# Weights of a fused retention and MLP kernel: loaded as fp32 by one queue and cast by GpSimd, instead of cast in flight by GpSimd's own queue

## The chip, the cores and the metric

The kernel runs on one core of a Trainium2 chip. The metric is the device time of one execution in microseconds (us). A core has five engines with queues of their own: TensorE (PE: matrix products), VectorE (DVE), ScalarE (ACT), GpSimd (POOL) and SyncE (SP, which here only issues DMAs). Sixteen DMA engines move the data of all queues.

## What is computed

Retention (attention with a decay in place of softmax) over 8 batches of 8 heads, 576 positions and 64 channels, then an MLP on the 4608 tokens:

```python
scores = scale * np.matmul(q, k.transpose(0, 1, 3, 2))
Dmat = np.where(rel >= 0, gamma[:, None, None] ** rel[None, :, :], 0.0)   # rel = position of query - of key
ret = scores * Dmat[None, :, :, :]
x = np.matmul(ret, v)            # then transposed to 4608 tokens x 512
h = x @ w_in                     # 512 x 2048
g = h * np.cos(h)
out = g @ w_out                  # 2048 x 512
```

All inputs and the output are fp32.

## The kernel before, in words

The decay is split into factors on q and v, so that the retention of a chunk of 128 positions is a masked product within the chunk plus a product with a running state. Batches 0 and 1 are worked in chunks of each batch (4 of 128 and one of 64 positions); from token 1152 on the chunks run over the joined sequence and are numbered by `g`, from 9 to 35. The MLP goes over nine blocks of 512 tokens: `mlp1` multiplies x by 128 columns of w_in (four products), ACT takes the cosine (`cb`, L552), DVE multiplies (`gt`, L554); the second product goes through `plain2` (blocks 0 and 1) or `mlp2` (the others). All products that are not woven go through `group` (L461, and L463 for a group's last), the woven ones of the later chunks through `weave` (L709).

All orders are written out by hand in `emit`: the calls stand there in one list, and each engine gets its instructions in that order and works them strictly in order. A small recorder adds semaphore waits.

Loads of q, k and v go to a ring of 16 buffers `ld` (128 x 512 fp32) and are issued by SP (`fetch`, L290; `load_g`, L317). A list of loads, `pend`, says in which order; `pump` is called after each use of a buffer and issues the next loads as long as their buffers are free. The loads of a joined chunk `g` are also held back when more than `AHEAD` (9) buffers would be in use, or `AHEAD + 3` from a certain `g` on. SP issues, in the same queue, the DMA transposes of the later chunks (`turn_dma`, L390), which bring k and q (`kq`) into the layout `kqt` that the scores need. `prep(g)` makes POOL cast k and scale q and v of chunk `g` (`casts_g`), then emits the transpose, then pumps; so where loads stand against transposes in SP's queue is set by that limit. `visit(g)` is PE's work on chunk `g` and the scores of chunk `g + 1`.

In batches 0 and 1 the first four chunks' k and q come as "quads" (`quad`, a load with rows of 256 values), are cast or scaled to `qs` (`quad_cast`), turned on PE and copied to `kqt`. `back` turns k back to `kq`, `scores` and its mask give `rt`, `state_mm` and `state_copy` keep the state (`st`, copied to `sb`), `rest` multiplies with v (`vb`, scaled by `decay`, L378) and copies x to `xt`.

The weights are loaded by POOL's queue in eight DMAs of 128 x 4 x 512 values each, four for w_in (L330) and four for w_out (L336), which convert fp32 to bf16 on the way into `win` and `wout`. They stand between POOL's scalings of batch 0's v. SP's loads of batch 0's last chunk and of batch 1 wait, by `after`, until the second of these has been issued in the program's order.

`idle(n)` issues n products of zeros on PE whose result nobody reads.

Of the kernel before, what the change touches and what calls it, by code (L numbers as in the profile page):

```python
# [12 lines left out]
DFF = 2048  # L13
DM = H_ * D_
# [9 lines left out]
NL = 16  # L24
AHEAD = 9
# [8 lines left out]
def slot(b, r):  # L34
    return SLOT[(NCH * b + r) % NR]
# [108 lines left out]
class _Kernel:  # L144
# [179 lines left out]
        src = bass.AP(self.src[x], (b * H_ + 2 * c) * S_ * D_, [[4 * D_, 128], [S_ * D_, 2], [1, 4 * D_]])  # L324
        self.fetch((x, b, "c", c), src, [[4 * D_, 2], [1, 4 * D_]], 128)

    def w_in_load(self, g):
        dst = bass.AP(self.WIN, 512 * g, [[4 * DFF, 128], [DFF, 4], [1, 512]])
        src = bass.AP(self.w_in, 512 * g, [[DFF, 128], [128 * DFF, 4], [1, 512]])
        self.wtok[f"wi{g}"] = self.s.dma("pool", f"wi{g}", lambda e: e.dma_start(dst, src), writes=[self.bWIN[g]])  # L330

    def w_out_load(self, g):
        dst = bass.AP(self.WOUT, 4 * g * DM, [[16 * DM, 128], [DM, 4], [1, DM]])
        src = bass.AP(self.w_out, 4 * g * 128 * DM, [[DM, 128], [128 * DM, 4], [1, DM]])
        w = Buf()
        t = self.s.dma("pool", f"wo{g}", lambda e: e.dma_start(dst, src), writes=[w])  # L336
        for i in range(4 * g, 4 * g + 4):
            self.bWOUT[i].w = [t]
        self.wtok[f"wo{g}"] = t

    def copy(self, eng, o, x, reads, writes):
        fn = (lambda e: e.activation(o, x, AF.Copy)) if eng == "act" else (lambda e: e.tensor_copy(o, x))  # L342
# [540 lines left out]
    def pump(self):  # L883

        while self.pend:
            fn, a = self.pend[0]
            if fn == self.after:
                if a[0] not in self.wtok:
                    return
            else:  # L890
                n = 3 if fn == self.load_g or fn == self.load and len(a) == 2 else 1
                if any(self.busy[(self.n_ld + i) % NL] for i in range(n)):
                    return
                if fn == self.load_g and sum(self.busy) + n > (AHEAD if a[0] < 4 * 4 else AHEAD + 3):
                    return
            self.pend.pop(0)
            fn(*a)

# [6 lines left out]
    def emit(self):  # L905
        self.late = None
        self.pend, self.wtok = [], {}
        self.busy = [False] * NL
        for b in range(2):
            if b:  # L910
                self.push(self.after, "wi1")
                self.push(self.load, 0, 4)
            for c in range(NP):
                for x in "kq":
                    self.push(self.quad, x, b, c)
            for r in range(4):
                self.push(self.load, b, r, "v")
        self.push(self.load, 1, 4)
        for g in range(G0, NG):
            self.push(self.load_g, g)  # L920
# [3 lines left out]
        def m1(dts, o, j=0):  # L924
            for dt in dts:
                self.mlp1(j, dt, *o)

        self.idle(10)
        for c in range(NP):
            for x in "kq":  # L930
                i = self.quad_cast("pool" if x == "k" else "dve", x, 0, c)
                self.pump()
                self.quad_turn(x, 0, c, i, "act")
                self.idle(2 if c else 1)
        self.s.need("pool", [self.wtok["v", 0, 0]])
# [7 lines left out]
        for r in range(4):  # L943
# [40 lines left out]
        def pairs(t):  # L984
            return [(t[i], int(t[i + 1])) for i in range(0, len(t), 2)]

        for n in range(16):
            self.plain2(0, n % 4, n // 4, None)
            if n == 3:
                self.turn(0, 4, "k", "act", PS)  # L990
                self.turn(0, 4, "q", "act", SS)
            if n == 4:
                self.scores(0, 4)
            if n == 6:
                self.rest(0, 4)
# [67 lines left out]
        for j in range(2, NTB):  # L1063
            g = 4 * j + 4 if j < NTB - 1 else NG
# [42 lines left out]
```

## Time and profile before

| | |
|---|---|
| median of 3 runs | 296.93 us (296.46 to 298.5) |
| the profiled execution | 299.12 us, span of its instructions 297.4 us |
| granted TensorE clock | 1.00 |
| busy, PE / DVE / ACT / POOL | 285.3 / 214.6 / 173.9 / 95.6 us |
| bytes read from HBM / written | 36.70 / 9.44 MB |
| weight loads, issue to landing (median) | w_in 10.2 us, w_out 17.0 us |

Times in the profile count from the span's start. A row of a time line has start, duration, engine, line, operation, result and sources, shape, how many instructions were merged, and in brackets the idle time of the engine just before and what ended it. "SPq" and "POOLq" rows are issues of DMAs: their duration is that of the issue, not of the transfer. A row of busy times by stage has the stage, then for each engine its busy time and, in brackets, its number of instructions, then the granted clock, the mean number of busy DMA engines as a share of 16 (over 1 where packets overlap), and GB/s. A row of the waits has the waiting engine and line, whom it waited for, the total, how many times, and the longest.

### The profile page before, as it was taken

How to read it: one execution, taken by the hardware profiler on the slowest of the kernel's cores; microseconds unless marked ns; L12 is line 12 of the kernel's file. 1: busy time of each engine (PE TensorE's matmuls, PEld its weight loads, DVE VectorE, ACT ScalarE, POOL GpSimd, SP SyncE). 2: the span in 40 equal slices, each digit the busy share in tenths (PEclk: the TensorE clock that was granted, in tenths of full speed). 3: DMA queues.
4: the chain of work that ended last, by engine and by line, in shares of the span. 5: the costliest groups of instructions: out<-in, count | busy, mean ns of one | idle time of the engine just before them, and what ended most of it. 6: DMA issues, size and time to landing. Idle time of an engine off the chain costs nothing.

```text
span 297.4 us, 8336 instructions
## 1 busy us (share of the span) xinstructions
PE 285.3 (96%) x3526; PEld 180.6 (61%) x3558; DVE 214.6 (72%) x465; ACT 173.9 (58%) x344; POOL 95.6 (32%) x120
## 2 busy tenths in 40 slices
PE   6899999999998999999999999999999999999996
PEld 2465455655553568646864785478547854785485
DVE  3667848568567688579857985798579757956973
ACT  6688624797347664566457535753586358535720
POOL 3580237754426430580058006700670030000000
PEclk9999999999999999999999999999999999999999
DMA  6999999999999999999999965899591170013013
GB/s 202 230 200 193 197 330 182 270 228 181 210 227 236 186 202 215 251 203 182 207 237 224 197 150 145 174 228 166 153 200 5 37 143 3 2 36 108 0 37 106
DMA packets 142325, 49.70 MB, mean 167 GB/s; under 512 B 125904, under 2 KB 141264, under 8 KB 142288
## 3 DMA queue, kind: packets, MB, share of 16 engines
q1 hardware_dynamic: 129280, 35.53, 67.3%
q10 hardware_dynamic: 8784, 9.44, 9.9%
q0 software_dynamic: 4224, 4.19, 8.7%
q8 instruction: 28, 0.46, 0.7%
q14 instruction: 9, 0.07, 0.1%
HBM read 36.70 MB, written 9.44 MB: 155 GB/s over the span
## 4 chain that ended last, share of the span: by engine, by line
PE 84%; DMA 9%; issue 2%; SPq 2%; DVE 1%; ACT 1%; DVEq 0%
PE mm L461 56%; PE mm L463 19%; DMA ld<-in_q_dram 3%; PE st L709 3%; PE sc L709 2%; DMA win<-in_moe_w_in_dram 2%; DMA ld<-in_v_dram 2%; DMA kqt<-kq 2%; SPq L290 2%; PE po L709 2%; PE sc L461 1%; PE po L461 1%; PE st L461 0%; PE sc L463 0%; ACT cb L552 0%
## 5 line engine op out<-in xcount | busy, mean ns | idle before, releaser
L554 DVE TENSOR_TENSOR gt<-mm,cb 128x512 bf16<-128x512 f32 (+3 forms) x156 | 99.4, 647 | 35.0 <-ACT cb L552 34.0
L552 ACT ACTIVATE cb<-mm,c_pih 128x512 bf16<-128x512 f32 (+3 forms) x156 | 100.7, 654 | 37.3 <-PE mm L463 36.4
L461 PE MATMUL mm<-xt,win 128*128 128x512 bf16 (+3 forms) x446 | 113.4, 362 | 3.1 <-issue 1.9
L461 PEld LDWEIGHTS mm<-xt,win 128*128 128x128 bf16 x468 | 43.5, 98 | 45.2 <-DVE gt L554 0.8
L463 PE MATMUL mm<-xt,win 128*128 128x512 bf16 (+3 forms) x156 | 56.6, 363 | 0.1
L342 POOL CAST kq<-ld 128x512 bf16<-128x512 f32 (+1 forms) x29 | 17.7, 610 | 117.4 <-PE mm L463 100.6
L461 PE MATMUL mm<-wout,gt 128*128 128x256 bf16 (+1 forms) x256 | 49.1, 309 | 1.0 <-issue 0.8
L461 PE MATMUL mm<-ts,ss 128*128 128x256 bf16 x240 | 35.4, 273 | 0.0
L461 PEld LDWEIGHTS mm<-wout,gt 128*128 128x128 bf16 x264 | 24.7, 98 | 11.8 <-DVE gt L554 0.5
L342 ACT ACTIVATE u<-mm 128x512 f32<-128x512 f32 x21 | 12.5, 597 | 32.3 <-PE mm L463 32.3
L365 POOL TENSOR_TENSOR vb<-ld,wv 128x512 bf16<-128x512 f32 x27 | 28.4, 1052 | 6.4 <-DMA ld<-in_v_dram 4.0
L361 POOL TENSOR_TENSOR kq<-ld,uq 128x512 bf16<-128x512 f32 x27 | 28.2, 1044 | 4.3 <-DMA ld<-in_q_dram 4.3
L342 ACT ACTIVATE xt<-po 128x256 bf16<-128x256 f32 (+1 forms) x35 | 14.6, 418 | 23.0 <-PE st L709 15.7
L463 PE MATMUL mm<-wout,gt 128*128 128x256 bf16 (+1 forms) x88 | 27.4, 311 | 0.1
L643 DVE TENSOR_TENSOR osb<-mm,u 128x512 f32<-128x512 f32 x20 | 13.8, 688 | 18.8 <-PE mm L463 11.2
L750 DVE TENSOR_TENSOR rt<-sc,mh 128x256 bf16<-128x256 f32 x54 | 21.2, 416 | 5.9 <-PE st L709 2.5
L463 PEld LDWEIGHTS mm<-xt,win 128*128 128x128 bf16 x156 | 15.3, 98 | 16.0
L461 PEld LDWEIGHTS mm<-ts,ss 128*128 128x128 bf16 x240 | 23.0, 98 | 2.8
L463 PE MATMUL mm<-ts,ss 128*128 128x256 bf16 x80 | 21.8, 272 | 0.0
L576 DVE TENSOR_TENSOR ss<-gt 128x512 bf16<-128x512 bf16 x56 | 20.7, 417 | 0.0
L760 DVE TENSOR_TENSOR pf<-sc,pf 128x256 f32<-128x256 f32 x42 | 17.6, 420 | 1.1
L709 PE MATMUL po<-rt,vb 64*64 64x64 bf16 x216 | 13.4, 202 | 0.1
(154 smaller groups left out, 386.6 us busy)
## 6 DMA issues: line engine op xcount, KB each, us to landing
out_dram<-osb ACTq DMA_DIRECT2D x35, 256.0 KB, 3.5
ld<-in_k_dram SPq DMA_DIRECT2D x32, 256.0 KB, 4.8
ld<-in_q_dram SPq DMA_DIRECT2D x32, 256.0 KB, 5.1
ld<-in_v_dram SPq DMA_DIRECT2D x32, 256.0 KB, 5.7
win<-in_moe_w_in_dram POOLq DMA_DIRECT2D x4, 512.0 KB, 10.2
wout<-in_moe_w_out_dram POOLq DMA_DIRECT2D x4, 512.0 KB, 17.0
ld<-in_k_dram SPq DMA_DIRECT2D x8, 128.0 KB, 4.5
ld<-in_q_dram SPq DMA_DIRECT2D x8, 128.0 KB, 4.0
```

The lines of the kernel that those rows point to most:

```text
L342: fn = (lambda e: e.activation(o, x, AF.Copy)) if eng == "act" else (lambda e: e.tensor_copy(o, x))
L361: self.s.op("pool", lambda e: e.tensor_tensor(o, a, w, ALU.mult), reads=[bt, self.bUQ], writes=[self.bQB[i]])
L365: self.s.op("pool", lambda e: e.tensor_tensor(o2, a2, w2, ALU.mult), reads=[bt, self.bWV], writes=[self.bVB[i]])
L461: self.nc.tensor.matmul(o, a, b, **kw)
L463: return s.done("pe", self.nc.tensor.matmul(o, a, b, **kw), reads, writes)
L552: s.op("act", lambda e: e.activation(ci, mi, AF.Sin, bias=self.C_PIH.ap(), scale=1.0), reads=[bm, self.bC], writes=[self.bCB[i]])
L554: s.op("dve", lambda e: e.tensor_tensor(bass.AP(self.GT, dt * TB + o0, [[16 * TB, 128], [1, n]]), mi, ci, ALU.mult), reads=[bm, self.bCB[i ...
L576: self.s.op("dve", lambda e: e.tensor_tensor(self.s_(k, d), a, b, op), reads=rd, writes=[S[k - 1][p]])
L643: self.s.op("dve", lambda e: e.tensor_tensor(o, m, x, ALU.add), reads=[bm, self.bU[u]], writes=[self.bOSB[i]])
L709: inst = self.nc.tensor.matmul(o, a, c, **kw)
L750: s.op("dve", lambda e: e.tensor_tensor(bass.AP(self.RT[n % 2][x], 0, p3), bass.AP(self.SC[x], 0, p3), bass.AP(self.MH, 0, [[64, 128], [0, ...
L760: s.op("dve", lambda e: e.tensor_tensor(self.PF[t].ap(), u, self.PF[1 - t].ap(), ALU.add), reads=[self.bSU[t], self.bPF[1 - t]], writes=[s ...
```

## The change

It has four parts. **The loads**: each weight piece is now four loads of 128 x 512 fp32 (256 KB, rows of 2 KB) into the ring `ld`, issued by SP; `w_cast` makes POOL cast each buffer to `win` or `wout`. **Their order**: w_in's first piece stands behind batch 0's second v; then v 2 and 3, the rest of w_in, two pieces of w_out, batch 0's chunk 4, w_out's third, batch 1's quads, w_out's last, batch 1's v. The wait `after` is gone. **The start of block 0**: `rest` of chunk 1 stands ahead of `back` of chunk 2 and its x is copied by ACT, not DVE; chunk 3's v is scaled by DVE, not POOL; two pairs of idle products go; the first two `mlp1` move ahead of chunk 2's state and output. **The limit**: `AHEAD + 3` holds from g = 18 on, not from 16.

```diff
-    def w_in_load(self, g):
-        dst = bass.AP(self.WIN, 512 * g, [[4 * DFF, 128], [DFF, 4], [1, 512]])
-        src = bass.AP(self.w_in, 512 * g, [[DFF, 128], [128 * DFF, 4], [1, 512]])
-        self.wtok[f"wi{g}"] = self.s.dma("pool", f"wi{g}", lambda e: e.dma_start(dst, src), writes=[self.bWIN[g]])
...
+    def w_load(self, x, g):
+
+        for c in range(4):
+            if x == "in":
+                src = bass.AP(self.w_in, 128 * c * DFF + 512 * g, [[DFF, 128], [1, 512]])
+            else:
+                src = bass.AP(self.w_out, (4 * g + c) * 128 * DM, [[DM, 128], [1, DM]])
+            self.fetch((x, g, c), src, [[1, DM]], 128)
+
+    def w_cast(self, eng, x, g, cs=range(4)):
+        for c in cs:
+            t, bt = self.use((x, g, c))
+            o = (bass.AP(self.WIN, c * DFF + 512 * g, [[4 * DFF, 128], [1, 512]]) if x == "in"
+                 else bass.AP(self.WOUT, (4 * g + c) * DM, [[16 * DM, 128], [1, DM]]))
+            u = self.copy(eng, o, t.ap(), [bt], [Buf()])
+            (self.bWIN[g] if x == "in" else self.bWOUT[4 * g + c]).w.append(u)
...
-                if fn == self.load_g and sum(self.busy) + n > (AHEAD if a[0] < 4 * 4 else AHEAD + 3):
+            if fn == self.load_g and sum(self.busy) + n > (AHEAD if a[0] < 4 * 4 + 2 else AHEAD + 3):
...
+        quads(0)
+        vs(0, range(2))
+        ws("in", [0])
+        vs(0, range(2, 4))
+        ws("in", range(1, 4))
+        ws("out", range(2))
+        self.push(self.load, 0, 4)
+        ws("out", [2])
+        quads(1)
+        ws("out", [3])
+        vs(1, range(4))
         self.push(self.load, 1, 4)
...
-        self.s.need("pool", [self.wtok["v", 0, 0]])
-        self.w_in_load(0)
         self.decay("dve", "v", 0, 0)
-        self.w_in_load(1)
-        for r in range(1, 4):
-            self.decay("pool", "v", 0, r)
-            if r < 3:
-                self.w_in_load(r + 1)
-        for r in range(4):
-            self.w_out_load(r)
+        self.decay("pool", "v", 0, 1)
+        self.w_cast("pool", "in", 0)
+        self.decay("pool", "v", 0, 2)
         self.pump()
...
+        self.rest(0, 1, self.bank(), state=False)
         self.back(0, 2, "act")
-        self.idle(2)
         self.state_mm(0, 1)
-        self.rest(0, 1, self.bank(), "dve", False)
         self.state_copy(1)
         self.scores(0, 3, False)
-        self.idle(2)
+        self.decay("dve", "v", 0, 3)
+        m1(range(2), (0, 256))
+        for g in range(1, 4):
+            self.w_cast("pool", "in", g)
+            self.pump()
+        for g in range(2):
+            self.w_cast("pool", "out", g)
+            self.pump()
         self.state_mm(0, 2)
         self.state_copy(2)
         self.rest(0, 2, state=False)
-        m1(range(2), (0, 256))
-        self.rest(0, 3, state=False)
-        m1(range(2, 4), (0, 256))
+        m1(range(2, 3), (0, 256))
+        self.rest(0, 3, self.bank(), state=False)
+        m1(range(3, 4), (0, 256))
         m1(range(3), (256, 256))
...
         self.casts(0, 4)
+        self.w_cast("pool", "out", 2)
         self.pump()
...
+            if n == 9:
+                self.w_cast("pool", "out", 3)
+                self.pump()
```

Three places show what this does to the engines' queues; line numbers after the change are 3 higher in these places. The first is ACT from the first copy of x on, in block 0's start: `xt` is x, `kq` k turned back, `sb` the state, `cb` the cosine of a piece of h. Before:

```order
L342 ACTIVATE xt<-po 128x4x128
L342 ACTIVATE kq2<-mm0 128x512
L342 ACTIVATE sb1<-st 64x4x64 x2
L342 ACTIVATE sb0<-st 64x4x64 x2
L342 ACTIVATE xt<-po 128x4x128
L552 ACTIVATE cb0<-mm0,c_pih 128x256
L552 ACTIVATE cb1<-mm1,c_pih 128x256
L342 ACTIVATE xt<-po 128x4x128
```

And after:

```order
L345 ACTIVATE xt<-po 128x4x128
L345 ACTIVATE xt<-mm0 128x4x128
L345 ACTIVATE kq2<-mm1 128x512
L345 ACTIVATE sb1<-st 64x4x64 x2
L555 ACTIVATE cb0<-mm0,c_pih 128x256
L555 ACTIVATE cb1<-mm1,c_pih 128x256
L345 ACTIVATE sb0<-st 64x4x64 x2
L345 ACTIVATE xt<-po 128x4x128
L555 ACTIVATE cb2<-mm2,c_pih 128x256
L345 ACTIVATE xt<-mm3 128x4x128
```

ACT gets chunk 1's copy of x as well, the first two cosines move ahead of chunk 2's state, and three cosines instead of two stand ahead of chunk 3's copy of x.

The second is POOL behind its last cast of batch 0's k. Before:

```order
L330 DMA win<-in_moe_w_in_dram 128x4x512 x2
L378 TENSOR_TENSOR vb1<-ld9,wv 128x512
L330 DMA win<-in_moe_w_in_dram 128x4x512
L378 TENSOR_TENSOR vb2<-ld10,wv 128x512
L330 DMA win<-in_moe_w_in_dram 128x4x512
L378 TENSOR_TENSOR vb3<-ld11,wv 128x512
L336 DMA wout<-in_moe_w_out_dram 128x4x512 x4
L342 COPY kq8<-ld12 64x512
```

And after, down to w_in's second piece:

```order
L381 TENSOR_TENSOR vb1<-ld9,wv 128x512
L345 COPY win<-ld10 128x512
L345 COPY win<-ld11 128x512
L345 COPY win<-ld12 128x512
L345 COPY win<-ld13 128x512
L381 TENSOR_TENSOR vb2<-ld14,wv 128x512
L345 COPY win<-ld0 128x512
L345 COPY win<-ld1 128x512
```

The issues of DMAs are gone from POOL, and one cast for each load stands in their place, w_in's first piece between the scalings of v 1 and 2.

The third is SP in the second block, from the transpose of chunk 12 (`kq8`) on; chunk 13 is `kq4`, chunk 14 `kq5`, and three loads are one chunk's k, q and v. Before:

```order
L390 DMA_TRANSPOSE kqt<-kq8 128x8x128
L317 DMA ld0<-in_k_dram 128x8x64
L317 DMA ld1<-in_q_dram 128x8x64
L317 DMA ld2<-in_v_dram 128x8x64
L317 DMA ld3<-in_k_dram 128x8x64
L317 DMA ld4<-in_q_dram 128x8x64
L317 DMA ld5<-in_v_dram 128x8x64
L390 DMA_TRANSPOSE kqt<-kq4 128x8x128
L317 DMA ld6<-in_k_dram 128x8x64
L317 DMA ld7<-in_q_dram 128x8x64
L317 DMA ld8<-in_v_dram 128x8x64
L390 DMA_TRANSPOSE kqt<-kq5 128x8x128
```

And after:

```order
L393 DMA_TRANSPOSE kqt<-kq8 128x8x128
L317 DMA ld0<-in_k_dram 128x8x64
L317 DMA ld1<-in_q_dram 128x8x64
L317 DMA ld2<-in_v_dram 128x8x64
L393 DMA_TRANSPOSE kqt<-kq4 128x8x128
L317 DMA ld3<-in_k_dram 128x8x64
L317 DMA ld4<-in_q_dram 128x8x64
L317 DMA ld5<-in_v_dram 128x8x64
L393 DMA_TRANSPOSE kqt<-kq5 128x8x128
L317 DMA ld6<-in_k_dram 128x8x64
L317 DMA ld7<-in_q_dram 128x8x64
L317 DMA ld8<-in_v_dram 128x8x64
```

Chunk 13's transpose has one chunk's loads ahead of it behind chunk 12's, where it had two; the second group of loads now stands behind it. Behind chunk 14's transpose two groups of loads follow where one did.

More of the change, by code (lines that the diff above doesn't have):

```diff
@@ L325, in quad @@
         self.fetch((x, b, "c", c), src, [[4 * D_, 2], [1, 4 * D_]], 128)
-    def w_in_load(self, g):
-        dst = bass.AP(self.WIN, 512 * g, [[4 * DFF, 128], [DFF, 4], [1, 512]])
-        src = bass.AP(self.w_in, 512 * g, [[DFF, 128], [128 * DFF, 4], [1, 512]])
-        self.wtok[f"wi{g}"] = self.s.dma("pool", f"wi{g}", lambda e: e.dma_start(dst, src), writes=[self.bWIN[g]])
[L332 to L339, printed above, removed]
+    def w_load(self, x, g):
[12 more added lines that the diff above has]
+            (self.bWIN[g] if x == "in" else self.bWOUT[4 * g + c]).w.append(u)
     def copy(self, eng, o, x, reads, writes):
@@ L886, in pump @@
             fn, a = self.pend[0]
[L887 to L893, printed above, removed]
-                if fn == self.load_g and sum(self.busy) + n > (AHEAD if a[0] < 4 * 4 else AHEAD + 3):
-                    return
+            n = 4 if fn == self.w_load else 3 if fn == self.load_g or fn == self.load and len(a) == 2 else 1
+            if any(self.busy[(self.n_ld + i) % NL] for i in range(n)):
+                return
+            if fn == self.load_g and sum(self.busy) + n > (AHEAD if a[0] < 4 * 4 + 2 else AHEAD + 3):
+                return
             self.pend.pop(0)
@@ L908, in emit, with quads @@
         self.busy = [False] * NL
[L909 to L912, printed above, removed]
+        def quads(b):
             for c in range(NP):
@@ L915, in emit, with vs, ws @@
                     self.push(self.quad, x, b, c)
-            for r in range(4):
+        def vs(b, rs):
+            for r in rs:
                 self.push(self.load, b, r, "v")
+        def ws(x, gs):
+            for g in gs:
+                self.push(self.w_load, x, g)
+        quads(0)
[9 more added lines that the diff above has]
+        vs(1, range(4))
         self.push(self.load, 1, 4)
@@ L934, in emit @@
                 self.idle(2 if c else 1)
-        self.s.need("pool", [self.wtok["v", 0, 0]])
-        self.w_in_load(0)
         self.decay("dve", "v", 0, 0)
-        self.w_in_load(1)
-        for r in range(1, 4):
-            self.decay("pool", "v", 0, r)
-            if r < 3:
-                self.w_in_load(r + 1)
-        for r in range(4):
-            self.w_out_load(r)
+        self.decay("pool", "v", 0, 1)
+        self.w_cast("pool", "in", 0)
+        self.decay("pool", "v", 0, 2)
         self.pump()
```

## The prediction

> **What bounds the kernel now.** I read the page first, then the busy times by stage, then the waits of TensorE (PE), then the time lines of single engines.
>
> ```profile
> PE 285.3 (96%) x3526; PEld 180.6 (61%) x3558; DVE 214.6 (72%) x465; ACT 173.9 (58%) x344; POOL 95.6 (32%) x120
> ...
> 0.00:19.00 19.00, 15.40 (x160) 7.79 (x162) 10.93 (x33) 12.51 (x24) 10.63 (x22) 1.00 0.93 211
> 19.00:57.00 38.00, 36.98 (x304) 20.35 (x310) 24.65 (x42) 22.60 (x43) 16.30 (x21) 1.00 1.15 228
> 57.00:115.00 58.00, 55.31 (x734) 32.09 (x741) 42.38 (x95) 38.03 (x80) 24.85 (x28) 1.00 1.23 214
> ...
> PE mm L461 <- issue: 2.7, 17, 0.2
> ...
> PE sc L709 <- DMA kqt<-kq: 1.3, 1, 1.3
> PE mm L461 <- POOL qs L342: 1.3, 1, 1.3
> ```
>
> PE is busy 96% of the span, at a granted clock of 1.00 in each stage. The 17 waits put down to "issue", 0.16 us each, are no loss: the groups behind them show two of three matmuls, so a record is missing. What can be won is therefore small and lies in few places: the start, stalls of tenths of a us before 57, and one wait of 1.3 us for a transpose. The DMA share of 1.15 and 1.23 says that the DMA engines are full from 19 to 115, so whatever moves loads can also cost.
>
> **Part 1, the start.** The first multiply of the MLP waits at 19.14 for w_in's first piece.
>
> ```profile
> 14.19 1.28 DVE L485 TENSOR_TENSOR rt<-mm,mk 128x512 bf16<-128x512 f32 x2
> 17.09 0.69 DVE L342 CAST xt<-mm 128x512 bf16<-128x512 f32 x1 [0.43 <-PE mm L463]
> ...
> 16.30 0.40 PE L461 MATMUL mm<-kqt,sb 128*128 128x128 bf16 x4
> 17.84 0.31 PE L461 MATMUL st<-vb,kq 128*64 128x64 bf16 x7
> 19.14 0.50 PE L461 MATMUL mm<-xt,win 128*128 128x256 bf16 x3 [0.31 <-DMA win<-in_moe_w_in_dram]
> 21.57 0.49 PE L461 MATMUL mm<-xt,win 128*128 128x256 bf16 x3
> ...
> 15.92 0.59 ACT L342 ACTIVATE kq<-mm 128x512 bf16<-128x512 f32 x1
> 16.41 0.78 ACT L342 ACTIVATE sb<-st 64x256 bf16<-64x256 f32 x2
> 18.20 0.78 ACT L342 ACTIVATE sb<-st 64x256 bf16<-64x256 f32 x2 [1.00 <-PE st L463]
> ...
> 19.79 0.91 ACT L552 ACTIVATE cb<-mm,c_pih 128x256 bf16<-128x256 f32 x2 [0.18 <-PE mm L463]
> 20.79 0.60 ACT L342 ACTIVATE xt<-po 128x512 bf16<-128x512 f32 x1
> ```
>
> Now the order. Chunk 1's product waits for its masks, which end at 14.19 + 1.28 = 15.47, and its result can be copied 0.79 later (16.30 to 17.09): at 16.26, by ACT now and not by DVE. From there ACT has to do, one behind the other, before the second 256 tokens can be multiplied: copy of x 0.5 (an instruction of 0.59 starts 0.49 before the next, 15.92 to 16.41), k 0.5, state 0.78, two cosines 0.91, state 0.78, x 0.5, one cosine 0.45, x 0.6: together 5.02, ending at 21.28. In the trace that last copy ends at 20.79 + 0.60 = 21.39, and the multiply follows at 21.57. So the first multiply moves about 2 us forward, to some 17.0, but ACT, which loses its 1.00 us of waiting and gets one more copy, holds the second half where it was. I take a gain of **0.1**. The upper end is ACT not pacing: 2.1 us less the state product and the output product that now stand behind the first multiply (17.84 to 19.14 less 0.31 of idle, 1.0), a gain of 1.1. The lower end is a loss of 0.4, if DVE's added scaling of chunk 3's v (0.69) and ACT come late by a copy. The four removed idle matmuls leave PE gaps of half a us here. In the trace a gap of 1.3 us, behind POOL's cast of qs in the start, left the clock of the stage at 1.00, so they are set at nothing.
>
> **Part 2, are the weights in time?** 32 loads of 256 KB take the place of eight on POOL's queue, in one row with all other loads, and POOL gets 32 casts.
>
> ```profile
> 6.97 0.62 POOL L342 CAST qs<-ld 128x512 bf16<-128x512 f32 x1 [2.67 <-DMA ld<-in_k_dram]
> ...
> 9.91 0.62 POOL L342 CAST qs<-ld 128x512 bf16<-128x512 f32 x1 [0.87 <-DMA ld<-in_k_dram]
> ...
> 11.72 0.69 DVE L378 TENSOR_TENSOR vb<-ld,wv 128x512 bf16<-128x512 f32 x1 [0.33 <-DMA ld<-in_v_dram]
> ...
> 47.61 3.16 POOL L378 TENSOR_TENSOR vb<-ld,wv 128x512 bf16<-128x512 f32 x3 [0.77 <-DMA ld<-in_v_dram]
> 50.98 1.04 POOL L378 TENSOR_TENSOR vb<-ld,wv 128x512 bf16<-128x512 f32 x1 [0.21 <-DMA ld<-in_v_dram]
> ...
> 23.94 0.59 PE L461 MATMUL mm<-xt,win 128*128 128x512 bf16 x2
> 37.98 0.26 PE L461 MATMUL po<-ident,kq 64*128 64x64 bf16 x3
> 49.41 0.81 PE L461 MATMUL mm<-wout,gt 128*128 128x512 bf16 x3
> ...
> ld<-in_k_dram SPq DMA_DIRECT2D x32, 256.0 KB, 4.8
> ```
>
> No load of fp32 weights with 2 KB rows is in the trace. The nearest rows are the k and q loads with rows of 1 KB: from 6.97 to 9.91 four of them land, 0.735 us each; rows of 256 bytes (v) take (50.98 - 47.61) / 3 = 1.12. Longer rows are nearer to the first, so I take 0.735 and keep 1.12 as the slow end. The second v then lands at 11.72 + 1.12 = 12.84, w_in's first piece, four loads, at 15.8, two v at 18.0, the other three pieces at 21.0, 23.9 and 26.8, w_out's first two at 29.8 and 32.7, batch 0's chunk 4 (three loads of half the size, 0.56 each) at 34.4, w_out's third at 37.3, batch 1's eight k and q loads at 43.2, w_out's last at 46.2. A cast adds 0.62 behind the last load. Against this stand the multiplies: w_in's second piece cast at 21.6 for 23.94; chunk 4's q (landed 33.8, scaled in 1.04) at 34.9 for the turn at 37.98; w_out's last at 46.8, or 47.3 with its four casts behind the k casts that wait for PE, for 49.41. The covers are 2.3, 3.0 and about 2 us, so PE waits for no weight and this costs **nothing**. POOL's 32 x 0.62 = 20 us fall where it idled (16.30 busy of 38); SP's own wait on casts is hidden by 16 buffers, some 10 us of loads in flight.
>
> **Part 3, batch 1's turns.** With loads of q late, PE stops between two turns.
>
> ```profile
> 42.59 0.33 PE L461 MATMUL po<-ident,qs 128*128 128x128 bf16 x3
> 42.81 0.33 PE L461 MATMUL st<-ident,qs 128*128 128x128 bf16 x3
> 43.90 0.33 PE L461 MATMUL sc<-ident,qs 128*128 128x128 bf16 x3
> 44.44 0.34 PE L461 MATMUL sc<-ident,qs 128*128 128x128 bf16 x3 [0.16 <-DVE qs L416]
> 45.54 0.33 PE L461 MATMUL po<-ident,qs 128*128 128x128 bf16 x3
> 45.98 0.34 PE L461 MATMUL st<-ident,qs 128*128 128x128 bf16 x3
> 47.08 0.33 PE L461 MATMUL sc<-ident,qs 128*128 128x128 bf16 x3
> 47.56 0.34 PE L461 MATMUL sc<-ident,qs 128*128 128x128 bf16 x3
> ...
> 46.81 0.69 DVE L416 TENSOR_TENSOR qs<-ld,uq 128x512 bf16<-128x512 f32 x1 [0.29 <-DMA ld<-in_q_dram]
> ```
>
> Two ready turns start 0.22 apart (42.59, 42.81); the next pairs are 0.54, 0.44 and 0.48 apart, so 0.32 + 0.22 + 0.26 = 0.80 us are lost, and DVE's scaling ahead of the last one waits until 46.81 for its load. By part 2 that load lands at 43.2, 3.6 us earlier, and the ones ahead of it by like amounts. I take a gain of **0.8**; the lower end is a loss, if loads come over 3.5 us later than worked out.
>
> **Part 4, the limit two chunks later.** In the trace the transpose of chunk 13 makes PE wait.
>
> ```profile
> 76.76 1.04 POOL L361 TENSOR_TENSOR kq<-ld,uq 128x512 bf16<-128x512 f32 x1 [0.17 <-DMA ld<-in_q_dram]
> ...
> 81.53 0.58 SPq L317 DMA_DIRECT2D ld<-in_k_dram  x1
> ...
> 91.10 2.84 SPq L390 DMA_TRANSPOSE kqt<-kq  x1
> ...
> 96.68 0.32 PE L709 MATMUL sc<-kqt 64*64 64x64 bf16 x16 [1.25 <-DMA kqt<-kq]
> ```
>
> Its q is ready at 77.80, but SP has the loads of chunks 15 and 16 ahead of it (81.53 to 91.10, six issues). Now only chunk 15's three stand ahead, half of the 9.57 us: it can go some 4.8 earlier, where 1.25 was wanted. What is late next: chunks 14 and 15 follow in SP's row with as many loads ahead as before or fewer, and chunk 14's is also freed by one group, so nothing is expected. I take a gain of **1.25**; the lower end is 0, if the profile's own disturbance made this wait. That is possible: the profiled execution took 299.12 us (span 297.4 and 1.72 around it), 2.2 over the median of 296.93.
>
> **Sum.** 0.1 + 0 + 0.8 + 1.25 = 2.15 us: the span goes to 295.25, the execution to 296.97, and the median, off which I take the same, from 296.93 to **294.8**.
>
> **Rivals.** *ACT does not pace the start*: the gain there is 1.1, the sum 3.15, the time 293.8. Against it, ACT idles for only 0.18 us between 18.20 and 20.79 already.
>
> *The stalls stay*: the transpose, or another one behind it, waits as before, because the DMA engines are full at a share of 1.23 whatever SP's order is; or the 1.25 us is not in undisturbed runs. Then 0.9 is left and the time is 296.0. This is also the case in which the new limit does not do what it says.
>
> *The weights come late* (slower): the loads stand in one row, so each k, q and v of batch 1 has 28 weight loads ahead of it. The place is chunk 4's q and batch 1's last q, the point about 0.87 us a load: 36 loads ahead of that q at 0.135 more each take 4.9 us, 1.3 beyond the 3.6 of lead, as much as parts 1 and 4 bring together. At 0.95 that q comes 7.7 later, 4.1 beyond its lead; less those 1.35 the time is 299.7, and at 1.12 (13.9 later) 305.9. Against it: 0.735 in the rows of shorter runs.
> [...]
>
> **How the numbers follow.** The forecast has a chance of 0.52 (its own range 294.0 to 295.7), ACT not pacing 0.16, the stalls staying 0.16, late weights 0.16. The range leaves out the last part of either side: from 293.4, somewhat below the best sum, to 299.0, inside the rival of late weights. A measurement here tells about 1% (3 us) from no change: faster than 294.0 is the second case and the edge of the first, 0.20; slower than 299.9 most of the last and odd cases, 0.15; the rest 0.65.
>
> **What would show it.** Part 1: first multiply near 17, but the second half's near 21.5, and ACT without gaps between. Part 2: POOL's casts of weights waiting for DMA, 0.6 to 0.8 apart, and no PE wait on a POOL cast of win or wout. Part 3: pairs of turns 0.22 apart. Part 4: no PE wait for kqt near 95. The prediction is wrong if weight loads land over 0.85 apart, if a new wait for kqt shows after 97, or if PE waits on POOL between 23 and 50.

## The result, and the profile after

| | before | after |
|---|---|---|
| median, 6 runs each | 297.28 us (296.46 to 298.5) | 300.59 us (299.68 to 301.29) |
| the profiled execution, its span | 299.12, 297.4 us | 300.25, 298.5 us |

The ratio after to before is 1.0094, 95% interval 1.0066 to 1.0123: slower by 0.9%, where 0.7% faster was forecast; the two medians by themselves give 1.011, inside that interval. Seven more runs beside a later set of experiments gave 1.0091 (1.006 to 1.0123). Ratios here and below leave out executions in a slower state, over 1.5% above the fastest of their kernel.

The page of the profile after has PE busier by 4.3 us. Of these 2.7 are records of PE that the profile before lacks (it has 3526 products, this one 3554), the waits there put down to "issue".

```profile
PE 289.6 (97%) x3554; PEld 180.8 (61%) x3554; DVE 216.1 (72%) x465; ACT 174.5 (58%) x345; POOL 108.3 (36%) x143
```

The same three stages as in the prediction:

```profile
0.00:19.00 19.00, 15.82 (x152) 8.15 (x154) 10.77 (x33) 13.28 (x25) 8.19 (x20) 1.00 0.88 240
19.00:57.00 38.00, 35.41 (x303) 18.64 (x304) 23.56 (x41) 21.10 (x40) 27.66 (x41) 1.00 1.07 294
57.00:115.00 58.00, 57.62 (x755) 32.61 (x750) 44.02 (x95) 38.27 (x81) 28.64 (x32) 1.00 1.18 224
```

From 57 on PE has next to no gap left (57.62 of 58 us; the kernel before had 55.31, of the difference 1.25 us are the wait for the transpose and 1.0 missing records). From 19 to 57 it has 2.6 us of them, and there the DMA engines are less busy than before: 1.07 where it was 1.15, and 0.88 in the first stage where it was 0.93. (The GB/s can't be compared with those before, where the weights are counted as bf16: 49.70 MB in packets, 53.89 now, with 36.70 MB read from HBM in both.) The waits of PE name the culprits: waits for POOL's casts of weights and for what stands behind these casts in POOL's row.

```profile
PE mm L464 <- POOL win L345: 1.0, 2, 0.6
PE st L464 <- POOL vb L381: 0.9, 2, 0.5
PE mm L464 <- POOL wout L345: 0.7, 1, 0.7
PE st L464 <- POOL kq L381: 0.6, 1, 0.6
```

Of the 1.0 us for `win` only 0.62 are for a weight: the other 0.43 stand ahead of a product without w_in, at 15.60, where eight other runs with this start have 0.4 us too, put down to DVE's masks. No DMA wait for `kqt` is among the waits of PE any more. The rows of PE's time line at these places:

```profile
17.34 0.50 PE L464 MATMUL mm<-xt,win 128*128 128x256 bf16 x3
...
18.90 0.31 PE L464 MATMUL st<-vb,kq 128*64 128x64 bf16 x7 [0.52 <-POOL vb L381]
...
21.79 0.49 PE L464 MATMUL mm<-xt,win 128*128 128x256 bf16 x3 [0.24 <-ACT xt L345]
...
24.63 0.82 PE L464 MATMUL mm<-xt,win 128*128 128x512 bf16 x3 [0.62 <-POOL win L345]
...
39.79 0.26 PE L464 MATMUL st<-ident,kq 64*128 64x64 bf16 x3 [0.60 <-POOL kq L381]
51.37 0.82 PE L464 MATMUL mm<-wout,gt 128*128 128x512 bf16 x3 [0.73 <-POOL wout L345]
52.77 0.31 PE L464 MATMUL st<-vb,kq 128*64 128x64 bf16 x7 [0.37 <-POOL vb L381]
...
57.15 0.82 PE L464 MATMUL mm<-wout,gt 128*128 128x512 bf16 x3
```

The last of these rows is block 0's last output product.

In POOL's time line the casts wait for DMAs. A row's bracket shows how long POOL idled for the load.

```profile
17.81 1.04 POOL L381 TENSOR_TENSOR vb<-ld,wv 128x512 bf16<-128x512 f32 x1 [0.53 <-DMA ld<-in_v_dram]
19.86 1.22 POOL L345 CAST win<-ld 128x512 bf16<-128x512 f32 x2 [1.01 <-DMA ld<-in_moe_w_in_dram]
21.62 0.61 POOL L345 CAST win<-ld 128x512 bf16<-128x512 f32 x1 [0.54 <-DMA ld<-in_moe_w_in_dram]
23.96 0.61 POOL L345 CAST win<-ld 128x512 bf16<-128x512 f32 x1 [1.73 <-DMA ld<-in_moe_w_in_dram]
24.81 3.24 POOL L345 CAST win<-ld 128x512 bf16<-128x512 f32 x5 [0.24 <-DMA ld<-in_moe_w_in_dram]
...
35.50 0.61 POOL L345 CAST wout<-ld 128x512 bf16<-128x512 f32 x1 [0.53 <-DMA ld<-in_moe_w_out_dram]
37.08 0.69 POOL L345 CAST wout<-ld 128x512 bf16<-128x512 f32 x1 [0.97 <-DMA ld<-in_moe_w_out_dram]
37.72 0.80 POOL L345 CAST kq<-ld 64x512 bf16<-64x512 f32 x1
38.70 1.04 POOL L381 TENSOR_TENSOR kq<-ld,uq 64x512 bf16<-64x512 f32 x1 [0.18 <-DMA ld<-in_q_dram]
...
50.70 0.61 POOL L345 CAST wout<-ld 128x512 bf16<-128x512 f32 x1 [0.15 <-DMA ld<-in_moe_w_out_dram]
```

So POOL is not too slow; the loads are late. Chunk 4's k landed at 37.45 and its q at 38.64, just ahead of their rows at 37.72 and 38.70; the prediction had q at 33.8. From the second piece on, the twelve loads of w_in and eight of w_out land between 18.44 (the last v) and 37.04: 0.93 us a load. Their spacing is not even: about half follow each other in 0.61 to 0.69 us, with gaps of up to 2.3 us in between. Against the prediction's row the fourth v is 0.4 us late (18.44 for 18.0), w_in's second piece already 2.9 (23.91 for 21.0), its last 3.1 (29.86 for 26.8), w_out's second 4.3 (37.03 for 32.7).

### The profile page after: what moved, and what is told of

The parts are those of the page before. It is cut to its first block, busy times and chain, and to the rows that moved or that the text cites. A ratio compares the mean times of both kernels' runs of the same rounds, so it can differ in the third digit from the quotient of the medians.

```text
span 298.5 us, 8413 instructions
## 1 busy us (share of the span) xinstructions
PE 289.6 (97%) x3554; PEld 180.8 (61%) x3554; DVE 216.1 (72%) x465; ACT 174.5 (58%) x345; POOL 108.3 (36%) x143
## 2 busy tenths in 40 slices
DMA packets 142709, 53.89 MB, mean 181 GB/s; under 512 B 126288, under 2 KB 137552, under 8 KB 142672
## 3 DMA queue, kind: packets, MB, share of 16 engines
HBM read 36.70 MB, written 9.44 MB: 155 GB/s over the span
## 4 chain that ended last, share of the span: by engine, by line
PE 81%; DMA 11%; SPq 3%; POOL 2%; issue 0%; DVE 0%; ACT 0%; DVEq 0%
PE mm L464 54%; PE mm L466 17%; DMA ld<-in_moe_w_in_dram 5%; DMA ld<-in_q_dram 3%; SPq L290 3%; PE st L712 3%; DMA ld<-in_v_dram 3%; PE sc L712 2%; PE po L712 2%; PE sc L464 1%; POOL wout L345 1%; PE po L464 1%; POOL vb L381 1%; PE sc L466 0%; POOL win L345 0%
## 5 line engine op out<-in xcount | busy, mean ns | idle before, releaser
L464 PE MATMUL mm<-xt,win 128*128 128x512 bf16 (+3 forms) x468 | 118.4, 363 | 1.3 <-POOL win L345 0.6
L466 PE MATMUL mm<-xt,win 128*128 128x512 bf16 (+3 forms) x156 | 56.6, 363 | 0.0
L464 PE MATMUL mm<-wout,gt 128*128 128x256 bf16 (+1 forms) x264 | 50.9, 312 | 0.8 <-POOL wout L345 0.7
L464 PE MATMUL mm<-ts,ss 128*128 128x256 bf16 x240 | 35.4, 273 | 0.0
L345 ACT ACTIVATE u<-mm 128x512 f32<-128x512 f32 x21 | 12.5, 597 | 32.3 <-PE mm L466 32.3
L345 ACT ACTIVATE xt<-po 128x256 bf16<-128x256 f32 (+1 forms) x34 | 14.0, 412 | 23.1 <-PE st L712 15.7
L466 PE MATMUL mm<-wout,gt 128*128 128x256 bf16 (+1 forms) x88 | 27.4, 311 | 0.0
L488 DVE TENSOR_TENSOR rt<-sc,mk 128x512 bf16<-128x512 f32 (+1 forms) x16 | 9.2, 615 | 6.3 <-PE sc L466 6.3
```

The lines of the kernel that those rows point to most:

```text
L464: self.nc.tensor.matmul(o, a, b, **kw)
L466: return s.done("pe", self.nc.tensor.matmul(o, a, b, **kw), reads, writes)
```

## The experiments

All ratios are to the kernel before in the same set of runs. "Over 0.25 us" counts the loads' packets of 1 KB or more that took longer than that between 16 and 28 us, worked out from the trace's packet records; the median there is 0.08 us for a packet of 2 KB.

### The kernel before again, and the limit alone

Two runs ask whether the transpose wait of the kernel before is a steady one, and what the limit brings by itself.

> The kernel before, once more, for a second look at its profile. Theory A (the 1.25 us wait of PE for a transpose near 95 us was an accident of the one profiled execution, which took 299.12 us against a median of 297.28): no wait for kqt over 0.3 us, a span near 295.5. Theory B (it is a steady part of the kernel): a wait of 0.8 us or more near 95 again. The ratio to before is 1.000 in either case.

Measured: 1.002 (0.9993 to 1.0048). Its profile has no PE stall between batch 1's turns, but it has the wait for the transpose again:

```profile
95.18 0.32 PE L709 MATMUL sc<-kqt 64*64 64x64 bf16 x16 [1.45 <-DMA kqt<-kq]
```

So the 1.25 us of part 4 was steady, and the 0.80 us of part 3 was in the one profiled execution and not in the other.

> The kernel before with the limit's change alone (AHEAD + 3 from chunk 18 on, not 16). Theory A: nothing to gain, ratio 0.999 to 1.001. Theory B: 1.25 us less, ratio 0.996. In both, chunk 13's transpose lands some 5 us ahead of its use.

```diff
-                if fn == self.load_g and sum(self.busy) + n > (AHEAD if a[0] < 4 * 4 else AHEAD + 3):
+                if fn == self.load_g and sum(self.busy) + n > (AHEAD if a[0] < 4 * 4 + 2 else AHEAD + 3):
```

Measured: 0.9946 (0.9922 to 0.9969), 1.6 us faster, with no `kqt` wait left. This one line, without the rest, beats both kernels. The rest of the change then costs 1.0094 / 0.9946 = 1.015, some 4.4 us.

### The limit taken back, and the old order of the start

> The changed kernel with the old limit (AHEAD + 3 from chunk 16 on). Theory A: no difference from the changed kernel, ratio to before 1.009. Theory B: the wait for chunk 13's transpose comes back, near 97, 1 us or more, ratio 1.013.

Edit: the diff above, reversed, in the changed kernel. Measured: 1.0177 (1.0128 to 1.0225). The wait for the transpose is back, and longer:

```profile
101.54 0.41 PE L712 MATMUL sc<-kqt 64*64 64x64 bf16 x16 [2.31 <-DMA kqt<-kq]
```

The limit does in the changed kernel what it does alone; the loss lies elsewhere.

> The changed kernel with block 0's start in the old order (chunk 1's x copied by DVE behind chunk 2's turn back, chunk 3's v scaled by POOL, the idle products, the first two multiplies behind chunk 2's output); weights and limit as changed. Forecast's part 1 (ACT holds the second half's multiplies in the new order, the first piece's landing in the old): the second half's first multiply moves by less than 0.4 us either way, ratio 1.007 to 1.011. Rival F (the new order itself costs): 1.5 us or more are won, ratio 1.004 or less.

```diff
-        self.rest(0, 1, self.bank(), state=False)
         self.back(0, 2, "act")
+        self.idle(2)
         self.state_mm(0, 1)
+        self.rest(0, 1, self.bank(), "dve", False)
...
-        self.decay("dve", "v", 0, 3)
-        m1(range(2), (0, 256))
+        self.idle(2)
+        self.decay("pool", "v", 0, 3)
...
+        m1(range(2), (0, 256))
+        self.rest(0, 3, state=False)
+        m1(range(2, 4), (0, 256))
```

Measured: 1.0122 (1.0081 to 1.0163), not better than the changed kernel. The comparison isn't clean, since the granted clock falls to 0.50 for 3.41 us in this run (see the last section); a run further down with the same order and no such fall has 1.0109. Taking the new order back wins nothing in either.

### What sets the weight loads' pace?

> The changed kernel with half of each weight load left out: rows of 1 KB, each cast twice into win or wout, so that as many loads, casts and cast bytes remain and the weights are wrong in half of their columns. Theory C: about 0.4 us a load, no wait of PE for a weight cast, for chunk 4 or for batch 1; ratio 0.994 to 0.997, that of the limit alone. Rival E (number of loads and casts, not bytes): 1.005 to 1.009.

```diff
-                src = bass.AP(self.w_in, 128 * c * DFF + 512 * g, [[DFF, 128], [1, 512]])
+                src = bass.AP(self.w_in, 128 * c * DFF + 512 * g, [[DFF, 128], [1, 256]])
```

(and the same for w_out; each loaded half is cast to both halves of the piece). Measured: 0.9934 (0.991 to 0.9958); no PE wait for a weight. Loads, casts and buffers are as many as in the changed kernel, so neither their number nor POOL's casts are the cost by themselves: the time that the transfers take is.

> The changed kernel with w_in read as 16 contiguous blocks of 128 x 512 instead of 128 rows of 2 KB that lie 8 KB apart: same bytes, same queues, same order (w_in's values are therefore permuted). Theory C (w_in's loads came late because reading rows 8 KB apart is slow: 0.99 us a load from 19.81 to 26.7 in the changed kernel, against 0.67 for w_out's contiguous ones): w_in's loads land 0.65 to 0.75 apart, PE's wait of 0.62 us near 24 goes, all that follows in the queue lands about 2 us earlier, and the waits of 0.60, 0.73 and 0.37 us near 39, 51 and 52 shrink below 0.2 each: ratio about 1.002 against 1.009 of the change. Rival D (the rate is set by SP, whose issues stood still for 3.21 us at 13.14 behind the descriptors of the v loads): landings and waits as in the changed kernel, ratio 1.009.

```diff
-                src = bass.AP(self.w_in, 128 * c * DFF + 512 * g, [[DFF, 128], [1, 512]])
+                src = bass.AP(self.w_in, (4 * g + c) * 128 * 512, [[512, 128], [1, 512]])
```

Measured: 1.0001 (0.9973 to 1.0028). Better, but not all: the wait for w_out at 49.8 stays (0.94 us), and 58 packets over 0.25 us are left, where the changed kernel's two profiles have 51 and 72. (Wait and packets are those of its longest execution, 300.34 us; its median is 298.34.) Neither theory fits: C had the waits under 0.2 us, D had no gain.

### Other orders and other queues

> The changed kernel with batch 0's chunk 4 (three loads of 128 KB, and their POOL work) ahead of w_out's first two pieces. Theory C: the wait of 0.6 us or more at chunk 4's turn near 39 goes, w_out's pieces come 2 to 2.5 us later and take part of it back; ratio 1.005 to 1.009 (0 to 1.2 us better than the change). Rival D (SP's issues, held up by loads of many short rows, set the pace): moving the short rows moves the hold-up ahead of w_out, PE waits for w_out near 35, ratio 1.009 or more.

```diff
-        ws("out", range(2))
         self.push(self.load, 0, 4)
+        ws("out", range(2))
...
+        self.casts(0, 4)
+        self.pump()
         self.state_mm(0, 2)
...
-        self.casts(0, 4)
```

Measured: 1.0115 (1.0076 to 1.0155). The wait for chunk 4 is gone and comes back for w_out:

```profile
38.55 0.82 PE L464 MATMUL mm<-wout,gt 128*128 128x512 bf16 x3 [2.92 <-POOL wout L345]
```

Another order only names another victim. This is what rival D said, the place (PE stops at 35.63) and the ratio included: chunk 4's three loads have 512 rows of 256 bytes each. Which loads are slow then is told under what stays open.

> The changed kernel with w_out loaded as before, by four DMAs of POOL's queue that convert in flight; w_in stays fp32 on SP's queue. Theory C (the single row of loads is what comes late: 28 weight loads of some 0.9 us stand ahead of batch 1's last q): with 16 of them on another queue chunk 4 and batch 1's k and q land 3 us or more earlier against their use, PE's waits near 39, 51 and 52 go, w_in's wait near 24 may stay; ratio 0.996 to 1.001. Rival E (POOL's casts of the weights, or the start's new order, make PE late): only the w_out casts go, ratio 1.005 or more.

Edit: w_out by POOL's queue as in the kernel before, cast in flight, w_in by SP's. Measured: 1.0175 (1.0136 to 1.0214). The forecast of a gain fell: w_in's last seven loads, which now shared the DMA engines with w_out's, landed 1.1 to 3.5 us apart, and PE waited 2.45 us for a cast of w_in at 30.70. The ratio is in rival E's range, but its mechanism isn't what the trace shows: POOL idles for the loads. Of the packets over 0.25 us 49 are SP's, 17 POOL's.

> The changed kernel, in which every second load of w_in's pieces 1 to 3 and of w_out's pieces 0 and 1 (ten loads) is issued by ACT's queue, all others by SP's as before. In the profiled changed kernel the DMA engines are busy for 0.93 of the stretch 18.5 to 30, and chunk 4's k lands at 37.45; in the kernel before, where two queues carry the loads, the share is 1.2. Theory G (one queue alone keeps the engines less busy than two): the share of that stretch rises to 1.1 or more, chunk 4's k lands before 36 us, and the waits for weights near 24 and 51 shrink. Rival (the rows of w_in 8 KB apart are slow in themselves, whichever queue carries them): the share stays at 0.93 to 1.0 and chunk 4's k lands at 37 or later. By both ACT pays for ten issues in the stretch that it paces (up to 0.4 us each), so that the first multiply of the first product comes later than 17.34, by up to 2 us, and the time alone decides little: 298 to 302 by G, 300 to 304 by the rival.

```diff
-            self.fetch((x, g, c), src, [[1, DM]], 128)
+            act = c % 2 and (x == "in" and g > 0 or x == "out" and g < 2)
+            self.fetch((x, g, c), src, [[1, DM]], 128, "act" if act else "sp")
```

Measured: 1.0245 (1.0222 to 1.0268). The stretch from 16 to 28 in the changed kernel, then here (clock, DMA share and GB/s are the last three numbers):

```profile
16.00:28.00 12.00, 10.52 (x118) 6.61 (x119) 6.92 (x15) 9.77 (x23) 7.11 (x11) 1.00 0.93 269
```

```profile
16.00:28.00 12.00, 8.81 (x104) 5.60 (x104) 4.33 (x8) 7.31 (x17) 7.77 (x13) 0.72 1.10 356
```

The loads do come faster (chunk 4's k at 33.87), not one of their packets in that stretch is over 0.25 us, and yet the kernel is slower, 304.95 us and so over both ranges: the ten issues stand in ACT's row (that they wait there for buffers is the author's reading), PE waits 3.79 us for ACT, and behind that wait the granted clock is 0.50 for 6.83 us.

```profile
17.45 0.29 PE L465 MATMUL st<-vb,kq 128*64 128x64 bf16 x7 [3.79 <-ACT kq L346]
```

By itself this run speaks for theory G, one queue too few, though the share of the stretch that was named, 18.5 to 30, came to 1.07 and not to 1.1; the last two experiments show that it was something else that ten loads on another queue avoid.

### The order of the start without the weight loads, and a filled wait

> The kernel before with its weights loaded and cast by POOL's queue as they were, the limit raised two chunks later, and the changed kernel's order of the start on PE and ACT (batch 0's fourth v on DVE, two groups of idle products gone, the first product's first multiplies ahead of state 2). If the new start is worth something by itself: the first multiply at 17.3 to 17.8 where the limit alone has 18.06, and a time 0.3 to 0.8 us under that of the limit alone, a ratio of 0.992 to 0.9935. Rival: the pieces of w_in by POOL's queue (17.61, 20.69, 23.23, 25.90 us landed with the limit alone) are then waited for, and the time is that of the limit alone, 0.9946, or longer.

Edit: the new order of the start and the new limit in the kernel before, weights by POOL's queue. Measured: 0.9985 (0.9965 to 1.0005). The rival held: the first multiply waits for w_in's first piece at 18.07, where the limit alone had it at 18.06 with other work in between, so the start lost its cover.

```profile
18.07 0.50 PE L461 MATMUL mm<-xt,win 128*128 128x256 bf16 x3 [1.53 <-DMA win<-in_moe_w_in_dram]
```

> The changed kernel with the old order of the start (ratio 1.0122), in which the 1.37 us wait of PE at 17.90 to 19.27 for batch 0's third v is filled with six idle products of 0.21 us. The wait's end stays where it is; only TensorE is kept busy through it. If the granted clock's 0.5 over 3.41 us behind that wait comes from the wait: it is gone, and with it about half of 3.41 us, 1.7 us, so the ratio falls to 1.006 to 1.008. If the half clock has another cause, or costs nothing since other work sets the pace there: the clock still falls, or the ratio stays at 1.010 to 1.014.

Edit: `idle(8)` for the `idle(2)` ahead of chunk 2's state in the run with the old start. Measured: 1.0109 (1.0076 to 1.0141). The half clock is gone (1.00 in all six runs, where three of the six with the old start had 0.994), but no gain can be told from 1.0122: the forecast of 1.006 to 1.008 fell.

> The changed kernel again, beside the others on one chip. By the theory (the weight loads come late in all its runs) the ratio is 1.007 to 1.012, with the waits for weights near 24 and 51 and for chunk 4's casts near 39, each 0.4 to 1 us, in the profile once more. Rival: the waits of the one profile were an accident of that run, as the kernel before's two turn stalls were; then they stand elsewhere or are under 0.3 us.

Measured: 1.0091 (1.006 to 1.0123). Waits of 0.72 and 1.16 us for chunk 4 near 38 and of 1.11 us for w_out at 51; the one for w_in near 24 is under 0.25. The places move a little, the lateness is steady: chunk 4's k landed at 37.31 (37.45 in the first profile).

### Short rows ahead of the weights

SP's time line shows how long issues take. In the changed kernel:

```profile
8.08 3.78 SPq L290 DMA_DIRECT2D ld<-in_moe_w_in_dram  x4
11.90 1.19 SPq L290 DMA_DIRECT2D ld<-in_v_dram  x2
13.13 10.08 SPq L290 DMA_DIRECT2D ld<-in_moe_w_in_dram  x12
```

Four loads of w_in take 3.78 us, although one takes 0.43 where nothing holds it, and twelve take 10.08. Within these rows single issues took 2.35, 3.21 and 1.35 us: each time the first behind batch 0's v, whose loads have 1024 rows of 256 bytes, or the next but one. The kernel before has such issues too (2.38 us for batch 0's third v), but no weight stands behind them on SP's queue.

> The changed kernel with batch 0's first four chunks of v read as 128 rows of 2 KB each where the kernel reads 1024 rows of 256 bytes; the bytes, loads and queue stay, and the values of these chunks are others. Theory H (the loads of many short rows hold up SP's issues, and the weight packets behind them on its queue are stuck for that): SP's hold-ups of 3.2 us at 13.1 and 1.35 us at 16.9 go, no more than a few packets over 0.25 us are left between 16 and 28, the weight loads land 0.65 to 0.68 us apart from the first on, chunk 4's k lands at 31 to 33.5 where the profiled changed kernel has 37.45, no wait of PE for weights is over 0.3 us, and the ratio is 0.994 to 1.000. Rival (w_in's rows 8 KB apart, or SP's queue as such): 30 or more such packets stay, chunk 4's k lands at 35.5 or later, ratio 1.004 to 1.010.

```diff
+            if b == 0 and r < 4 and x == "v":
+                self.fetch((x, b, r), bass.AP(self.src[x], CH * r * DM, [[DM, CH], [1, DM]]), [[1, DM]], CH)
+                continue
             self.fetch((x, b, r), src, [[D_, H_], [1, D_]], ck)
```

Measured: 0.9949 (0.9928 to 0.997). Theory H holds at nearly all points (not in the even spacing: a gap of 2.2 us stays at 18.89, and w_out's last loads ahead of chunk 4 land 0.9 us apart). SP:

```profile
5.86 2.02 SPq L290 DMA_DIRECT2D ld<-in_moe_w_in_dram  x4
7.92 1.03 SPq L290 DMA_DIRECT2D ld<-in_v_dram  x2
8.99 6.12 SPq L290 DMA_DIRECT2D ld<-in_moe_w_in_dram  x12
```

The DMA engines between 16 and 28:

```profile
16.00:28.00 12.00, 11.58 (x103) 6.80 (x103) 8.06 (x16) 10.57 (x24) 9.47 (x16) 1.00 1.05 385
```

And POOL, now without a gap of over 0.4 us from 19 to 39:

```profile
16.04 1.29 POOL L348 CAST win<-ld 128x512 bf16<-128x512 f32 x2 [0.22 <-DMA ld<-in_moe_w_in_dram]
18.95 6.72 POOL L348 CAST win<-ld 128x512 bf16<-128x512 f32 x10 [1.61 <-DMA ld<-in_moe_w_in_dram]
25.73 3.31 POOL L348 CAST wout<-ld 128x512 bf16<-128x512 f32 x5
...
32.19 0.61 POOL L348 CAST kq<-ld 64x512 bf16<-64x512 f32 x1 [0.35 <-DMA ld<-in_k_dram]
33.09 1.04 POOL L384 TENSOR_TENSOR kq<-ld,uq 64x512 bf16<-64x512 f32 x1 [0.29 <-DMA ld<-in_q_dram]
```

One queue alone moves 385 GB/s here, where the same queue with the same bytes moved 269. Chunk 4's k comes at 32.15, 5.3 us earlier, q 5.6 earlier. One gap of 1.61 us is left at 18.95.

Two things in these 5.3 us aren't hold-ups: batch 0's last k lands earlier in this profile (at 8.61, not 9.89), and the loads of v take less time themselves. Counted from the landing of the second v, chunk 4's k comes 25.1 and 25.4 us later in the changed kernel's two profiles, and 21.3 us later here (20.3 in the next run). Of these 4 to 5 us the other two v account for 0.5 to 0.8 by their own transfers (1.4 us for both, not 1.8 and 2.1).

What the lateness costs can be read in PE's row, from the first multiply of block 0's second half to block 0's last output product:

```profile
20.07 0.49 PE L467 MATMUL mm<-xt,win 128*128 128x256 bf16 x3 [0.24 <-ACT xt L348]
...
52.41 0.82 PE L467 MATMUL mm<-wout,gt 128*128 128x512 bf16 x3
```

These are 32.3 us, the same within 0.01 in the kernel before's second profile, with the limit alone, with start and limit, with half the bytes and in both runs with long rows. In the changed kernel's two profiles they are 35.4 and 36.1 (21.79 to 57.15 in the first).

> As the run before, and w_in read from contiguous memory too, 128 rows of 2 KB side by side (values of w_in's pieces and of the four chunks of v are others). By theory H nothing is added: the ratio is that of the run before within 0.003, 0.993 to 1.000. By the rival in which w_in's rows make the stuck packets, this run is well under the run before, by 0.005 or more, and at 1.000 as with a contiguous w_in alone or under it. If stuck packets stay here too, neither kind of rows makes them, and it is SP's queue with 24 loads in a row.

Edit: that of the run before and that of the contiguous w_in together. Measured: 0.9946 (0.9929 to 0.9963). Nothing is added: w_in's rows 8 KB apart cost nothing that can be measured once v's short rows are gone. The gain of a contiguous w_in alone (1.0001 against 1.0094) is thus one that only shows behind the short rows.

| | loads of batch 0's v | packets over 0.25 us, longest | chunk 4's k landed | ratio |
|---|---|---|---|---|
| changed kernel (two profiles) | 1024 short rows | 51 (1.89 us), 72 (1.35 us) | 37.45, 37.31 | 1.0094 |
| w_in contiguous | 1024 short rows | 58 (0.73 us) | 35.7 | 1.0001 |
| half of each weight load | 1024 short rows | 34 (0.75 us) | 28.53 | 0.9934 |
| every second weight by ACT | 1024 short rows | 0 | 33.87 | 1.0245 |
| long rows of v | 128 long rows | 2 (0.29 us) | 32.15 | 0.9949 |
| long rows of both | 128 long rows | 0 | 31.98 | 0.9946 |

## Why the prediction was wrong, point by point

**Part 1, the start: right.** The first multiply is at 17.34 ("to some 17.0"), the second half at 21.79 where it was 21.57; the second profiles of both kernels have it at 20.83 and 20.73. ACT paces it, with two small gaps:

```profile
16.37 0.60 ACT L345 ACTIVATE xt<-mm 128x512 bf16<-128x512 f32 x1 [0.31 <-PE mm L466]
...
19.26 0.78 ACT L345 ACTIVATE sb<-st 64x256 bf16<-64x256 f32 x2 [0.28 <-PE st L466]
...
21.04 0.60 ACT L345 ACTIVATE xt<-mm 128x512 bf16<-128x512 f32 x1
```

Its last copy starts at 21.04 and ends at 21.64, 0.25 later than before; 21.28 was worked out. One reservation: idle products were set at nothing, and in the run of start and limit alone a wait of 1.53 us stood where they and the work moved had been, and the second half started at 21.95, 1.4 us later than with the limit alone.

**Part 2, the weights in time: this step failed.** It said that weights take 0.735 us a load, that "PE waits for no weight and this costs nothing". They took 0.93 from the second piece on, and PE waits between 17 and 53 for what hangs on them: 0.52, 0.62, 0.60, 0.73 and 0.37 us, 2.8 in all. It wasn't the price of a load with long rows: in undisturbed stretches that is 0.67 to 0.69 (w_out's first five, 30.80 to 33.52 in the changed kernel), under what was taken. What failed is the way in which the loads of one queue were added up. A load of short rows was charged with its own time (1.12 us for a v) and nothing else, while the loads around it are late too. Behind v SP's issues are held up for 1.35 to 3.21 us, and packets of the weights behind take up to 1.89 us instead of 0.08. Giving v long rows takes 1.0094 to 0.9949, 4.3 us, as much as the 4.4 that the changed loads and start cost. By the profiles the lateness behind the start accounts for 3.0 to 3.8 us of it (32.3 against 35.4 and 36.1), and with long rows none of it is left. The rest lies in the start itself, whose second half begins at 21.79 and 20.83 in the changed kernel and at 20.07 and 20.89 with long rows, and that differs between profiles of one kernel by as much.

The rival "the weights come late" had the place (chunk 4's q, w_out) and, at 0.95 us a load, the time: 299.7, with 300.59 measured. Its cause was not in it: it took a higher price of every load.

**Part 3, batch 1's turns: wrong, in part for an accident.** The 0.80 us of stalls weren't in the kernel before's second profile, so there was little to gain. Batch 1's last q came at 47.85, 4.7 us later than worked out. The pairs of turns are 0.22 to 0.38 apart even so, since PE came to them 1.7 us later.

**Part 4, the limit: right.** 1.25 us were forecast, the limit alone brought 1.6 (0.9946), and no new wait for a transpose came.

With long rows of v, which bring other values, the whole change came to 0.9949, with 0.993 forecast. That nearness would have been luck: the limit alone gives 0.9946, and the sum's other gains, 0.1 and 0.8, aren't in it.

**What stays open**: how the short rows make other loads slow. The runs show only that between 16 and 28 us short rows of v and slow packets come and go together on one queue, that half of the weight loads on ACT's queue show none, and that a contiguous w_in and half loads suffer less in time from as many or somewhat fewer. Elsewhere slow packets come with long rows of v too, 19 between 8 and 12 us in one run and 16 between 28 and 32 in the other. Nor are only the loads behind late: the four loads of w_out just ahead of chunk 4's short rows land at 33.52, 34.31, 35.45 and 37.03 in the changed kernel. With chunk 4 moved ahead of w_out, it is w_in's last that land far apart (24.42, 26.48, 28.23, 29.28, 30.14, 31.28), and w_out's first twelve follow 0.66 to 0.70 apart. Short rows of v issued by a queue of their own, and long rows of v in the kernel before, weren't tried.

## What to carry to other kernels

Before loads are put into one queue with others, look not only at how long those transfer but at how many rows they have: here the loads of 1024 rows of 256 bytes charged the loads around them with more than their own 1.1 us (from the second v to chunk 4's k 25.1 and 25.4 us passed, with long rows 21.3). Look at the queue's own row of issues: here issues of 2.35 and 3.21 us, where 0.43 was usual, were the sign; the kernel before had one of 2.38 too, with no weight behind it on that queue. And take a stall for gain only if a second profile has it: of two kinds of stall that the prediction counted, one was steady and one was gone.

## What the runs showed of the hardware

The issue of a load wasn't of constant cost in these runs. Twelve issues of 128 rows took 10.08 us behind loads of short rows and 6.12 without them; on SP's queue, which carries these loads, one issue behind two loads of 1024 rows took 3.21 us, where the median of w_in's sixteen is 0.43.

In one run the clock fell after a short wait: with the old start PE waits 1.37 us, and 0.4 us behind it the granted clock falls to 0.50 for 3.41 us:

```profile
19.26 0.31 PE L464 MATMUL st<-vb,kq 128*64 128x64 bf16 x7 [1.37 <-POOL vb L381]
```

```profile
19.64:23.05 3.41, 3.41 (x30) 2.35 (x30) 0.51 (x2) 2.28 (x5) 2.42 (x4) 0.50 0.91 317
```

The same came 0.1 to 1.0 us behind waits of 2.31 (limit taken back), 2.45 (w_out by POOL) and 2.92 us (chunk 4 first), and not behind those of 1.45 (kernel before) and 1.53 us (start and limit), whose profiled executions have a clock of 1.00. So length alone didn't decide in these runs. Half of 3.41 us, 1.7, is an estimate of the most that one such fall costs, if half the clock doubles all of PE's times; filling the wait of 1.37 us with idle products kept the clock at 1.00 without a gain that could be measured.
